# New prices and ranks for the planner of an expert stage, and the last tile's scaling moved behind a branch

## The chip, the cores and the metric

The kernel runs on one core of one Trainium2 chip. The metric is the time of one execution on the device in microseconds, the median of three runs. Five engines work side by side and wait for one another through semaphores: TensorE (PE in the profile; PEld is its loading of weights), VectorE (DVE), ScalarE (ACT), GpSimd (POOL) and SyncE (SP, which here only issues DMAs).

## The reference

Three layers over 2304 tokens of width 512, cut to what matters. All weights and activations are float32.

```python
def reference(...):
    attn = attention(q, k, v, M_prev, z_prev, beta)   # 4 batches, 8 heads, 576 tokens, d 64
    x = attn.transpose(0, 2, 1, 3).reshape(2304, 512)
    # mixture of 8 experts: each token goes to one
    logits = x @ w_gate
    e = argmax(logits, axis=1); gate_w = softmax(logits)[e]
    y = gate_w * (relu(x @ w1[e]) @ w2[e])             # w1 512x1024, w2 1024x512
    # a dense pair of layers
    h = y @ w_in                                       # 512x2048
    return where(h > 0, h, exp(min(h, 0)) - 1) @ w_out # 2048x512
```

## The kernel before

Three stages follow one another, and each is planned apart. The attention ends near 208 us, the expert stage runs to about 498 us, the dense stage takes the rest.

**The expert stage** (`moe`, L1213) works on tiles of 128 tokens, sorted by expert. The program has 23 fixed tiles (`NTM`, numbers 0 to 22). Two more (`NTM` to `NT`) stand in a branch, `tc.If(nt > NTM)` at L1752, that is entered only if the tokens fall so unevenly over the experts that more than 23 tiles are needed; it isn't entered with these inputs. One tile is: fetch 128 rows by index (`gather`, L1172, on POOL), transpose them on PE (L1276), split into a high and a low part (L1197 to L1203), 24 matmuls with w1 (L1337), relu on ACT (L1347, called h), transpose h (L1362), split, 24 matmuls with w2 (L1380), scale by the gate weight (L1393 on ACT or L1396 on DVE), and scatter the rows with an indirect DMA (L1423, after L1419 has put the tokens' numbers beside them).

**Weights.** If a tile has another expert than the tile before it, `tile_weights` (L1158) loads w1 in two DMAs of 1 MB and w2 in two more, and `wsplit` splits them: four steps on ACT (L1312, two casts of 128x1024 each) and four on DVE (L1317, two subtractions each). If it has the same expert, a flag that the chip itself works out makes SP, ACT and DVE jump over that (the branches at L1310 and L1315). So each of these steps is in the program for every tile from 1 on, and whether it costs anything is known on the chip alone.

**Beside the tiles** the stage does three other things: the routing of the last batch (`gate_plan` and `routing`, a chain of small steps on DVE and PE that tells tiles 4 to 22 their tokens), the repacking of the dense stage's weights (`Widen`: 32 parts, each a load into `wide`, one step on ACT at L1116, four on DVE at L1120 to L1132, and a store to `wf`), and the first three loads of these weights back (`first`, L1439).

**What sets the order.** A planner (`Plan`) is given all operations of a stage, each with the engines that may run it, a cost in ns, what it reads and writes, a rank (`prio`, lower goes first) and, for DMAs, a time in a common queue. It plays them through in time: at each step it takes the engine that can start first, and among the operations that can start within `slack` of that the one with the lowest rank. The order so found is each engine's program; on the chip every engine then goes through its own list strictly in order. A tile's rank is 1000 times its number, plus a constant for the kind of operation, plus an offset from the table `moff` in `KNOBS` (for instance "1t2" for the matmuls with w1 of tile 2). `K["load"]` is the DMA time that the planner books for one `tile_weights` call of a tile (default `m_ld`, 3500), `K["same"]` what it books for one weight-splitting step on ACT and on DVE (default `m_if`, 700). Both had own values for tiles 1 to 3 only. "late" and "late2" are the ranks of the last batch's gate and routing. Buffers and PSUM banks are handed out by the same play-through (`Ring`, `Slot`); `released` tells the order in which the PSUM banks come free, and the dense stage takes them in that order.

**The end of the stage.** The last tile's result goes into a bank of the ring for w1's products and is scaled into a corner of a weight buffer. Its scaling, number copy and scatter are part of the plan; the branch at L1752 stands behind the plan in the source.

Of the kernel before, what the change touches and what calls it, by code (L numbers as in the profile page):

```python
# [32 lines left out]
NTM = NT - 2  # L33
# [86 lines left out]
class Plan:  # L120
# [144 lines left out]
KNOBS = {  # L265
    "xe": ("ACT", "DVE"), "he": ("ACT",), "re": [("ACT",), ("ACT", "DVE")], "m_ld": 3500.0, "m_x": -2208.9, "m_1": -1447.9, "m_h": -4434.5, "m_lag": 0.0,
    "m_if": 700.0, "m_fl": -3000.0, "m_wl": 300.0, "wa": 0, "wa0": 10022.449169040721, "wa1": 23927.854833523612, "wt": 1, "wp": 16, "wj": 2000.0,
    "m_g": -500, "wq": 0.64, "sa": 95.3, "sm": 0.0, "s2": 150.0, "hd": -807380.0, "mem": -2415304.4, "xg": 4,
    "wh": [("ACT", "DVE"), ("ACT", "DVE"), ("ACT", "DVE"), ("DVE",), ("ACT",), ("ACT", "DVE"), ("ACT", "DVE"), ("ACT", "DVE")],
    "wl": [("DVE",), ("DVE",), ("DVE",), ("DVE",), ("DVE",), ("DVE",), ("DVE",), ("DVE",)], "ord": [3, 4, 2, 1, 0], "rings": 4, "ab": 2, "nq": 2,  # L270
    "nv": 2, "na": 2, "na4": 2, "nx": 2, "nls": 2, "wide": 1, "de": ("DVE", "POOL"), "busy": [0, 0, 0], "early": -250015.8, "late": 4025.2,
    "late2": 5033.0, "mld": -1956.4, "gate": -150617.9, "warm": [52, 0.0, 200.0], "qe": ("DVE",),
    "off": {"tk": 566796.0, "tq": 730416.0, "hk": -153830.8, "hq": 102000.2, "px": -706093.7, "phi": -153683.4, "S3": -519297.9, "S4": -875790.6, "S2": -808121.2, "S1": -886679.1, "S0": -903722.2, "min3": -650466.1, "min4": -656196.4, "min2": 99641.2, "min1": 773227.1, "min0": -808922.5, "exp3": 834197.7, "exp4": -1722599.5, "exp2": 566072.9, "exp1": 893897.4, "exp0": 608896.6, "T3": 570667.0, "T4": 691939.6, "T2": 562700.4, "T1": 104395.2, "T0": 95607.6, "Te3": -1956.7, "Te4": -370288.3, "Te2": 703913.6, "Te1": 683059.5, "Te0": -888022.2, "fin": -51043.5, "mm": -162856.2, "md": -261207.1, "ms": 171709.6, "avA": -370579.0, "avB": 171831.9, "ave": -150657.8, "rw": -1189064.1, "ls": -697154.8, "add": -705115.8},
    "es": {"x": ("ACT",), "T0": ("ACT", "DVE"), "T3": ("ACT", "DVE"), "k": ("ACT", "DVE"), "T1": ("ACT",), "T4": ("ACT", "DVE"), "q": ("ACT",), "T2": ("ACT", "DVE")},
    "glag": {3: 6500.0}, "begin": {"PE": 300.0, "DVE": 2100.0}, "load": {1: 100.0, 2: 5240.0, 3: 100.0},
    "same": {1: (150.0, 150.0), 2: (1950.0, 2450.0), 3: (150.0, 150.0)},
    "moff": {"x0": 13435.3, "xe0": 22685.2, "fACT0": 17446.5, "fDVE0": 18937.6, "1t0": -19968.7, "r0t0": 11469.5, "r1t0": 8016.8, "h0t0": -12050.5, "h1t0": -7987.2, "he0t0": 10156.1, "he1t0": -756.6, "2t0": -1051.8, "yt0": -3878.6, "w0t0": 4525.5, "w1t0": 19974.4, "w2t0": -21470.7, "w3t0": 59.3, "w4t0": 4555.4, "w5t0": 13589.9, "w6t0": 22393.4, "w7t0": 15561.2, "x1": -1076.0, "xe1": -5940.5, "fACT1": -5210.8, "fDVE1": -246.9, "1t1": -8238.6, "r0t1": 20652.8, "r1t1": -9722.7, "h0t1": -14320.2, "h1t1": 4359.4, "he0t1": -566.2, "he1t1": -2023.2, "2t1": 7927.9, "yt1": 4658.9, "sh0t1": 4642.7, "sh1t1": 6076.0, "sh2t1": 11617.3, "sh3t1": 17594.9, "sl0t1": -800.3, "sl1t1": -8451.5, "sl2t1": -4070.1, "sl3t1": 3393.0, "x2": 4431.3, "xe2": -1464.8, "fACT2": 4958.1, "fDVE2": 5793.9, "1t2": 19111.1, "r0t2": 4317.1, "r1t2": 13362.6, "h0t2": -4316.7, "h1t2": -7360.8, "he0t2": 1487.7, "he1t2": 2315.0, "2t2": 3316.2, "yt2": 11174.7, "sh0t2": 7463.8, "sh1t2": 11468.1, "sh2t2": 19952.2, "sh3t2": 3089.1, "sl0t2": 4551.9, "sl1t2": -15052.7, "sl2t2": 19969.9, "sl3t2": 18614.4, "x3": 6545.5, "xe3": -14606.2, "fACT3": 6360.6, "fDVE3": 4604.0, "1t3": 6547.4, "r0t3": 13373.7, "r1t3": 32874.8, "h0t3": 3850.6, "h1t3": -6823.9, "he0t3": -6525.6, "he1t3": 4650.0, "2t3": -4197.2, "yt3": 13940.6, "sh0t3": 16527.2, "sh1t3": 18722.6, "sh2t3": -18207.3, "sh3t3": -12155.8, "sl0t3": 2292.5, "sl1t3": -5211.1, "sl2t3": 11196.1, "sl3t3": -6237.2},
    "wait": 25, "first": 1042461.7, "stick": 1109662.3,
}

# [215 lines left out]
def ca(n, sb=False, bias=False, acc=False):  # L496
    if acc:
        return 240 + 0.833 * n
    return (110 if sb else 65) + 0.833 * n


def cv(n):
    return 70 + 1.04 * n
# [709 lines left out]
def moe(tc, c, w1, w2, tiles):  # L1213
    nc = tc.nc
    mp, pl, K = c.mp, c.pl, c.K

    def sb(name, n, shape, dt=F32, more=()):
        if name not in c.mt:
            c.mt[name] = [*more] + [mp.tile(shape, dt, name=f"{name}{i}") for i in range(n)]
        return Ring(name, c.mt[name])  # L1220
# [30 lines left out]
    def mtile(t):  # L1251
        pr = 1000.0 * t

        def at(x, y):
            return pr + y + K["moff"].get(f"{x}{t}", 0.0)
# [3 lines left out]
        sg = Slot(r_xg)  # L1259
        if t:  # L1260
            for j in range(2):
                if t == 1 and j == 1:

                    def f():
                        for w in raw[2:]:
                            nc.gpsimd.memset(w[0:1, 0:1], 0.0)
                    pl.op("POOL", 150, f, w=[("raw", 1, 2), ("raw", 1, 3)], prio=pr + K["m_g"])
                tile_weights(tc, c, (w1, w2), t, j, prio=pr - 2900 + 900 * j, dma=K["load"].get(t, K["m_ld"]))
            gather(tc, c, t, lambda: sg.t, r=[("tok", part)] + ([("xd", B - 1)] if part else []), w=[sg], prio=pr - 3000, lag=K["glag"].get(t, 0.0))
        else:  # L1270
            sg.index = r_xg.free.pop(0)[1]
# [115 lines left out]
        if t == NTM - 1:  # L1387
            def f():
                nc.gpsimd.memset(sy.t[:, DM:], 0.0)
            pl.op("POOL", 100, f, w=[("raw", 0, 0), (sy, "id")], prio=pr)  # L1390

        def fa():
            nc.scalar.activation(sy.t[:, 0:DM], y.t, AF.Copy, scale=sg.t[:, DM:DM + 1])  # L1393
# [1 line left out]
        def fv():  # L1395
            nc.vector.tensor_scalar_mul(sy.t[:, 0:DM], y.t, sg.t[:, DM:DM + 1])  # L1396
        es = ("ACT", "DVE") if t < NE else ("ACT",)
        pl.op(es, [{"ACT": ca(512), "DVE": cv(512)}[x] for x in es], [{"ACT": fa, "DVE": fv}[x] for x in es], r=[y, sg], w=[sy], prio=at("yt", 500))

        if t < NE - NY:  # L1400
            def f():
# [13 lines left out]
                  K["he"], ("DVE",))  # L1415
            return

        def f():
            nc.gpsimd.tensor_copy(sy.t[:, DM:DM + 1], c.R.tok[part][:, t - NE:t - NE + 1])  # L1419
        pl.op("POOL", 100, f, r=[sy, ("tok", part)], w=[(sy, "id")], prio=pr + 499)  # L1420

        def f():
            ins = nc.gpsimd.indirect_dma_start(out=c.yd[:, :], out_offset=bass.IndirectOffsetOnAxis(ap=c.R.pos[:, t - NE:t - NE + 1], axis=0),  # L1423
                                               in_=sy.t, in_offset=None, bounds_check=NTOK - NE * P - 1, oob_is_err=False)
            c.no_dep(ins, "y")
        pl.op("POOL", 1040, f, r=[sy, (sy, "id"), "pos", "ypad"], w=[], prio=pr + 500, dma=728, lag=K["m_lag"])

    for t in tiles:
# [216 lines left out]
def kernel(ctx, tc, q, k, v, M_prev, z_prev, beta, w_gate, w1, w2, w_in, w_out, out):  # L1645
# [17 lines left out]
    def released(tiles, rings):  # L1663
        return [next(i for i, x in enumerate(tiles) if x is r.tiles[k]) for _, _, k, r in sorted((t, n, k, r) for n, r in enumerate(rings) for t, k in r.free)]
# [29 lines left out]
    with ExitStack() as s1:  # L1694
# [25 lines left out]
                    wd.part(n, c.K["wa0"] + c.K["wa1"] * n)  # L1720
            phase(build, c.K["sa"], 0.0, **BEGIN)
        with ExitStack() as s2:
            c.mt = {}
            c.mp = Singles(tc, s2)
            c.qone = counts(c.mp, 768)
            for n, k in (("h", 2), ("hh", 2), ("hl", 2)):
# [68 lines left out]
```

## Time and profile before

| | us |
|---|---|
| median of three runs | 912.38 |
| the runs | 911.12 to 916.92 |
| the profiled execution | 913.57 |
| its span, first to last instruction | 911.8 |

The profile is of one execution. The span is what its instructions cover; 1.77 us of the execution lie outside it. A row of the timeline gives start, duration, engine, line of the source, operation, what is written and read, and in brackets how long the engine had stood idle and what it waited for. "x4" means four instructions shown as one row.

### The profile page before, as it was taken

How to read it: one execution, taken by the hardware profiler on the slowest of the kernel's cores; microseconds unless marked ns; L12 is line 12 of the kernel's file. 1: busy time of each engine (PE TensorE's matmuls, PEld its weight loads, DVE VectorE, ACT ScalarE, POOL GpSimd, SP SyncE). 2: the span in 40 equal slices, each digit the busy share in tenths (PEclk: the TensorE clock that was granted, in tenths of full speed). 3: DMA queues.
4: the chain of work that ended last, by engine and by line, in shares of the span. 5: the costliest groups of instructions: out<-in, count | busy, mean ns of one | idle time of the engine just before them, and what ended most of it. 6: DMA issues, size and time to landing. Idle time of an engine off the chain costs nothing.

```text
span 911.8 us, 19048 instructions
## 1 busy us (share of the span) xinstructions
PE 887.9 (97%) x7397; PEld 737.7 (81%) x7397; DVE 571.0 (63%) x1045; ACT 402.5 (44%) x793; POOL 114.2 (13%) x176
## 2 busy tenths in 40 slices
PE   8999999999999999999999999999999999999996
PEld 5777777778788888888887899888888888888895
DVE  5878797979755686468996874444444345344442
ACT  6888888886433574358875331111111112111110
POOL 1111111130001122232111000010001000100100
PEclk9999999999999999999999999999999999999998
DMA  6435353367436883789974620110001000000000
GB/s 120 97 90 130 80 132 69 93 213 243 142 108 220 328 264 129 239 312 372 332 272 171 223 98 13 36 47 0 24 24 47 1 23 24 36 1 1 35 13 23
DMA packets 97108, 110.04 MB, mean 121 GB/s; under 512 B 65390, under 2 KB 65390, under 8 KB 94704
## 3 DMA queue, kind: packets, MB, share of 16 engines
q1 hardware_dynamic: 90992, 95.26, 32.7%
q0 software_dynamic: 4800, 13.18, 4.2%
q8 instruction: 59, 0.97, 0.4%
q10 hardware_dynamic: 1216, 0.30, 0.1%
q14 instruction: 41, 0.34, 0.1%
HBM read 87.94 MB, written 23.41 MB: 122 GB/s over the span
## 4 chain that ended last, share of the span: by engine, by line
PE 68%; DMA 2%; DVE 1%; ACT 1%; issue 0%; POOLq 0%; SPq 0%; POOL 0%; ACTq 0%; DVEq 0%
PE ptt L1607 22%; PE ptt L1582 21%; PE pmt L1380 12%; PE pmt L1337 11%; PE pmt L1362 2%; PE pmt L1276 1%; DMA wide<-wf 1%; DMA half<-wf 1%; PE ptt L1549 1%; DMA ex<-xd,r_tok 0%; DVE wq L1317 0%; ACT h L1347 0%; DVE w L1496 0%; POOLq L1791 0%; ACT wq L1312 0%
## 5 line engine op out<-in xcount | busy, mean ns | idle before, releaser
L1590 ACT ACTIVATE elu<-ptt 128x512 f32<-128x512 f32 x72 | 42.9, 598 | 315.9 <-PE ptt L1582 315.9
L1594 DVE TENSOR_SCALAR elu<-elu 128x512 f32<-128x512 f32 x72 | 31.0, 430 | 187.9 <-ACT elu L1590 187.9
L1607 PE MATMUL ptt<-w,gh 128*128 128x512 f32 x432 | 134.7, 393 | 0.0
L1380 PE MATMUL pmt<-w,hh 128*128 128x512 f32 x368 | 125.0, 400 | 0.0
L1607 PEld LDWEIGHTS ptt<-w,gh 128*128 128x128 f32 x432 | 79.3, 188 | 15.2
L1607 PE MATMUL ptt<-w,gl 128*128 128x512 f32 x216 | 84.2, 390 | 0.0
L710 ACT ACTIVATE a<-pat,st 128x128 f32<-128x128 f32 (+2 forms) x144 | 78.2, 548 | 8.6 <-DVE st L705 5.4
L1380 PEld LDWEIGHTS pmt<-w,hh 128*128 128x128 f32 x368 | 69.1, 188 | 13.4 <-DVE w L1317 0.2
L705 DVE TENSOR_REDUCE st<-pat 128x2 f32<-128x256 f32 (+4 forms) x80 | 64.0, 800 | 19.9 <-PE pat L687 16.5
L1380 PE MATMUL pmt<-w,hl 128*128 128x512 f32 x184 | 71.8, 390 | 0.0
L1582 PE MATMUL ptt<-yTh,w 128*128 128x256 f32 (+1 forms) x288 | 68.8, 318 | 0.0
L1496 DVE TENSOR_TENSOR gl<-tnh,gh 128x512 fp32r<-128x512 f32 x72 | 49.9, 693 | 5.1 <-PE ptt L1607 0.5
L1598 DVE SCALAR_TENSOR_TENSOR tnh<-ptt,elu 128x512 f32<-128x512 f32 x72 | 49.8, 692 | 4.5 <-DVE elu L1594 0.5
L1582 PEld LDWEIGHTS ptt<-yTh,w 128*128 128x128 f32 x288 | 49.2, 190 | 4.0
L827 POOL TENSOR_TENSOR raw<-ms,ls 128x80 f32<-128x80 f32 (+2 forms) x45 | 30.3, 696 | 140.7 <-DVE ls L815 134.6
L1607 PEld LDWEIGHTS ptt<-w,gl 128*128 128x128 f32 x216 | 40.6, 188 | 8.7
L683 PE MATMUL pat<-ab 64*128 64x128 f32 (+3 forms) x256 | 47.0, 473 | 0.2 <-ACT ab L633 0.2
L1582 PE MATMUL ptt<-yTl,w 128*128 128x256 f32 (+1 forms) x144 | 45.8, 318 | 0.0
L1203 DVE TENSOR_TENSOR hl<-pmt,hh 128x512 fp32r<-128x512 f32 x46 | 31.6, 687 | 20.1 <-ACTq L1310 13.2
L1197 ACT CAST hh<-pmt 128x512 fp32r<-128x512 f32 x46 | 27.3, 593 | 36.8 <-PE pmt L1380 28.9
L1347 ACT ACTIVATE h<-pmt 128x512 f32<-128x512 f32 x46 | 27.1, 597 | 37.2 <-PE pmt L1337 35.9
L117 PE MATMUL pat<-ident,a 64*128 64x64 f32 x800 | 36.8, 229 | 5.2 <-ACT a L710 3.9
(343 smaller groups left out, 1932.7 us busy)
## 6 DMA issues: line engine op xcount, KB each, us to landing
wraw<-in_moe_w_dram SPq DMA_DIRECT2D x24, 1024.0 KB, 7.0
wrbw<-in_moe_w_dram SPq DMA_DIRECT2D x12, 1024.0 KB, 7.8
wide<-in_moe_w_in_dram SPq DMA_DIRECT2D x16, 512.0 KB
wf<-half SPq DMA_DIRECT2D x32, 256.0 KB, 4.2
wide<-in_moe_w_out_dram SPq DMA_DIRECT2D x16, 512.0 KB
wide<-wf SPq DMA_DIRECT2D x9, 512.0 KB, 8.4
v<-in_v_dram SPq DMA_DIRECT2D x32, 128.0 KB, 2.9
wraw<-yd SPq DMA_DIRECT2D x14, 258.0 KB, 2.5
```

Source lines behind the costliest of these rows:

```text
L117: nc.tensor.transpose(out, x, ident[hs, hs])
L683: nc.tensor.matmul(s.t[:, 512 * h:512 * h + n], row(1)[hs, i * P:(i + 1) * P], row(0)[hs, 0:n], start=True, stop=False)
L705: nc.vector.tensor_reduce(ss.t[:, 2 * i:2 * i + (2 if i < 4 else 1)], src(), axis=AX.X if i < 4 else AX.XY, op=ALU.min)
L710: nc.scalar.activation(sa[i].t[:, h, :] if i < 4 else sa[4].t[:, 0:S].rearrange("p (y n) -> p y n", y=2), src()[:, h, :] if i < 4 else src ...
L1203: nc.vector.tensor_sub(lo(), src(), hi().bitcast(F32))
L1337: nc.tensor.matmul(g[hf].t, a.t[:, cc, :], b[:, 512 * hf:512 * (hf + 1)], start=(cc == 0 and n == 0), stop=(cc == 3 and n == 2))
L1380: nc.tensor.matmul(y.t, a.t[:, 2 * (q % 2) + jj, :], b[:, 512 * jj:512 * (jj + 1)], start=(q == 0 and jj == 0 and n == 0), stop=(q == 3 an ...
L1496: nc.vector.tensor_sub(lo(), src(), hi().bitcast(F32))
L1582: nc.tensor.matmul(h.t[:, n * j + n0:n * j + n1], w(cc, a, ft), b(cc), start=(cc == 0 and x == 0), stop=(cc == 3 and x == 2))
L1590: nc.scalar.activation(se.t, h.t, AF.Exp)
L1598: nc.vector.scalar_tensor_tensor(st.t, h.t, 0.0, se.t, op0=ALU.max, op1=ALU.add)
L1607: nc.tensor.matmul(acc[a].t, y.t[:, n * j + P * a:n * j + P * (a + 1)], wsub(1, k, ft // 2)[:, ft % 2, :], start=(ft == 0 and x == 0), sto ...
```

## The change

It has five parts, all for the expert stage.

1. Prices. `load` and `same` get own values for tiles 4 to 22 too. Tiles 9, 10, 16, 17, 19, 20 and 22 are booked as new experts (5240 ns of DMA for each of the two `tile_weights` calls, 1950 and 2300 ns for each splitting step on ACT and DVE), the other twelve as repeated ones (100 and 150).
2. Ranks. All offsets in `moff` for tiles 0 to 3 are new, and tiles 4, 20, 21 and 22 get offsets for the first time. The planner's `slack` in this stage (`sm`) goes from 0 to 30 ns, "late" from 4025.2 to 5288.6 and "late2" from 5033.0 to 7126.8.
3. A new memset of one element on POOL, which tile 2's first weight load then waits for.
4. The last tile's scaling, number copy and scatter leave the plan and are issued behind the branch, in the order copy, scaling, scatter.
5. What these three read is held: the PSUM bank of the last result stays taken in the plan and is put at the end of the list that the dense stage takes its banks from, and the row buffer is withheld from the rare tiles.

```diff
-"sm": 0.0, ... "late": 4025.2, "late2": 5033.0,
+"sm": 30.0, ... "late": 5288.6, "late2": 7126.8,
-"load": {1: 100.0, 2: 5240.0, 3: 100.0},
-"same": {1: (150.0, 150.0), 2: (1950.0, 2450.0), 3: (150.0, 150.0)},
+"load": {1: 100.0, 2: 5240.0, 3: 100.0, 4: 100.0, ... 9: 5240.0, 10: 5240.0, ... 22: 5240.0},
+"same": {1: (150.0, 150.0), 2: (1950.0, 2450.0), ... 9: (1950.0, 2300.0), ... 22: (1950.0, 2300.0)},
-"moff": {"x0": 13435.3, ... "1t2": 19111.1, ... "sl3t3": -6237.2},
+"moff": {"x0": 22273.2, ... "1t2": 44312.7, ... "sl3t4": 4255.9, "x20": -14925.1, ... "sl3t22": 6770.1},
@@ moe
+    if c.held is not None:
+        r_xg.free = [x for x in r_xg.free if x[1] != c.held.index]
@@ mtile
+                if t == 2 and j == 0:
+                    def f():
+                        nc.gpsimd.memset(raw[0][0:1, 0:1], 0.0)
+                    pl.op("POOL", 100, f, w=[("raw", 0, 0)], prio=pr - 2950)
@@ t == NTM - 1
             pl.op("POOL", 100, f, w=[("raw", 0, 0), (sy, "id")], prio=pr)
+            y.left += 1
+            c.held = sg
-        pl.op(es, [...], [{"ACT": fa, "DVE": fv}[x] for x in es], r=[y, sg], w=[sy], prio=at("yt", 500))
+        if t != NTM - 1:
+            pl.op(es, [...], [{"ACT": fa, "DVE": fv}[x] for x in es], r=[y, sg], w=[sy], prio=at("yt", 500))
-        pl.op("POOL", 100, f, r=[sy, ("tok", part)], w=[(sy, "id")], prio=pr + 499)
+        if t == NTM - 1:
+            c.tail = [fi, fa, f]
+            return
+        pl.op("POOL", 100, fi, r=[sy, ("tok", part)], w=[(sy, "id")], prio=pr + 499)
@@ tile_attention_moe_mlp_kernel
             late = released(ones, (c.rg, c.rt, c.ry))
+            late += [k for k in range(8) if k not in late]
             nt = nc.values_load(...)
             with tc.If(nt > NTM):
                 ...
+            with tc.manual_schedule():
+                for f in c.tail:
+                    f()
```

## Rows read from the trace of the kernel before

**Rows 1.** The page's first part: busy time, share of the span, instructions.

```profile
PE 887.9 (97%) x7397; PEld 737.7 (81%) x7397; DVE 571.0 (63%) x1045; ACT 402.5 (44%) x793; POOL 114.2 (13%) x176
```

**Rows 2.** Windows of the expert stage; the first row names the columns.

```profile
core 0: us, PE busy (x) PEld busy (x) DVE busy (x) ACT busy (x) POOL busy (x), PEclk, DMA share, GB/s
...
410.00:420.00 10.00, 9.48 (x46) 7.95 (x47) 9.81 (x14) 9.34 (x13) 1.36 (x2) 1.00 1.03 387
...
450.00:460.00 10.00, 10.00 (x47) 8.31 (x46) 9.93 (x12) 8.11 (x12) 3.20 (x3) 1.00 1.01 384
...
480.00:490.00 10.00, 8.89 (x44) 7.11 (x43) 5.24 (x8) 4.23 (x7) 1.35 (x2) 1.00 0.72 262
```

**Rows 3.** Waits of PE, 205 to 520 us: us in total, times, longest.

```profile
PE pmt L1362 <- ACT h L1347: 2.1, 3, 1.1
```

**Rows 4.** The chain that ended last, one undisturbed tile: start us, us, what.

```profile
313.23 4.80 PE pmt L1380 x21
...
325.50 4.79 PE pmt L1380 x21
```

**Rows 5.** Timeline of ACT and of PE around the stalls at 410 and 435 us.

```profile
409.31 0.67 ACT L1116 ACTIVATE half<-wide 128x512 f32<-128x512 f32 x1 [1.73 <-DMA wide<-in_moe_w_out_dram]
...
410.52 0.66 PE L1362 MATMUL pmt<-ident,h 128*128 128x128 f32 x4 [0.66 <-ACT h L1347]
...
433.78 1.25 ACT L1116 ACTIVATE half<-wide 128x512 f32<-128x512 f32 x2
...
435.57 0.66 PE L1362 MATMUL pmt<-ident,h 128*128 128x128 f32 x4 [0.29 <-ACT h L1347]
```

**Rows 6.** Timeline and chain around the stall at 486 us.

```profile
477.45 7.14 DMA wide<-wf
...
484.77 1.04 ACT L1197 CAST wraw1n<-wide 128x1024 fp32r<-128x1024 f32 x1 [2.00 <-DVEq L1315]
...
486.36 1.15 PE L1362 MATMUL pmt<-ident,h 128*128 128x128 f32 x8 [1.11 <-ACT h L1347]
```

**Rows 7.** One splitting step on ACT and DVE (timeline); weight loads (page, part 6).

```profile
427.17 2.00 ACT L1312 CAST w<-wrbw 128x1024 fp32r<-128x1024 f32 x2
...
431.12 2.36 DVE L1317 TENSOR_TENSOR w<-wrbw,w 128x1024 fp32r<-128x1024 f32 x2 [0.45 <-ACT w L1312]
...
wraw<-in_moe_w_dram SPq DMA_DIRECT2D x24, 1024.0 KB, 7.0
wrbw<-in_moe_w_dram SPq DMA_DIRECT2D x12, 1024.0 KB, 7.8
```

**Rows 8.** Timeline of PE and POOL: the stage's first matmuls; tile 4's rows.

```profile
207.65 3.22 PE L1337 MATMUL pmt<-wq,x 128*128 128x512 f32 x12
...
244.91 1.19 POOL L1172 DMA_INDIRECT ex<-xd,r_tok  x1 [32.97 <-DVE r_past L1069]
...
248.57 0.72 PE L1276 MATMUL pmt<-ident,ex 128*128 128x128 f32 x4 [0.60 <-DMA ex<-xd,r_tok]
```

**Rows 9.** Lines L1752 and L1393 (duration ns min/median/max, first and last start); timeline 494 to 509 us.

```profile
L1752 ACTq COMPARE_BRANCH  x1: 50/50/50, 494.0 to 494.0; - x1
...
L1393 ACTq EVENT_SEMAPHORE  x22: 17/38/510, 226.3 to 496.1; - x22
...
494.77 0.50 POOL L1419 CAST wraw<-r_tok 128x1 f32<-128x1 uint32 x1
...
497.91 0.69 ACT L1393 ACTIVATE wraw<-pmt,xs 128x512 f32<-128x512 f32 x1 [2.04 <-PE pmt L1380]
498.66 1.06 PE L1549 MATMUL ptt<-ident,wraw 128*128 128x128 f32 x8 [0.79 <-ACT wraw L1393]
498.67 0.98 SPq L1508 DMA_DIRECT2D half<-wf  x2
```

**Rows 10.** Timeline of POOL and SP at the stage's start.

```profile
205.79 0.09 POOL L1266 MEMSET wrbw<- 1x1 f32 x1
...
206.08 7.31 SPq L1158 DMA_DIRECT2D wraw<-in_moe_w_dram  x2
```

More of the change, by code (lines that the diff above doesn't have):

```diff
@@ L267 @@
     "m_if": 700.0, "m_fl": -3000.0, "m_wl": 300.0, "wa": 0, "wa0": 10022.449169040721, "wa1": 23927.854833523612, "wt": 1, "wp": 16, "wj": 2000.0,
-    "m_g": -500, "wq": 0.64, "sa": 95.3, "sm": 0.0, "s2": 150.0, "hd": -807380.0, "mem": -2415304.4, "xg": 4,
+    "m_g": -500, "wq": 0.64, "sa": 95.3, "sm": 30.0, "s2": 150.0, "hd": -807380.0, "mem": -2415304.4, "xg": 4,
     "wh": [("ACT", "DVE"), ("ACT", "DVE"), ("ACT", "DVE"), ("DVE",), ("ACT",), ("ACT", "DVE"), ("ACT", "DVE"), ("ACT", "DVE")],
@@ L270 @@
     "wl": [("DVE",), ("DVE",), ("DVE",), ("DVE",), ("DVE",), ("DVE",), ("DVE",), ("DVE",)], "ord": [3, 4, 2, 1, 0], "rings": 4, "ab": 2, "nq": 2,
-    "nv": 2, "na": 2, "na4": 2, "nx": 2, "nls": 2, "wide": 1, "de": ("DVE", "POOL"), "busy": [0, 0, 0], "early": -250015.8, "late": 4025.2,
-    "late2": 5033.0, "mld": -1956.4, "gate": -150617.9, "warm": [52, 0.0, 200.0], "qe": ("DVE",),
+    "nv": 2, "na": 2, "na4": 2, "nx": 2, "nls": 2, "wide": 1, "de": ("DVE", "POOL"), "busy": [0, 0, 0], "early": -250015.8, "late": 5288.6,
@@ L273 @@
+    "late2": 7126.8, "mld": -1956.4, "gate": -150617.9, "warm": [52, 0.0, 200.0], "qe": ("DVE",),
     "off": {"tk": 566796.0, "tq": 730416.0, "hk": -153830.8, "hq": 102000.2, "px": -706093.7, "phi": -153683.4, "S3": -519297.9, "S4": -875790.6, "S2": -808121.2, "S1": -886679.1, "S0": -903722.2, "min3": -650466.1, "min4": -656196.4, "min2": 99641.2, "min1": 773227.1, "min0": -808922.5, "exp3": 834197.7, "exp4": -1722599.5, "exp2": 566072.9, "exp1": 893897.4, "exp0": 608896.6, "T3": 570667.0, "T4": 691939.6, "T2": 562700.4, "T1": 104395.2, "T0": 95607.6, "Te3": -1956.7, "Te4": -370288.3, "Te2": 703913.6, "Te1": 683059.5, "Te0": -888022.2, "fin": -51043.5, "mm": -162856.2, "md": -261207.1, "ms": 171709.6, "avA": -370579.0, "avB": 171831.9, "ave": -150657.8, "rw": -1189064.1, "ls": -697154.8, "add": -705115.8},
@@ L274 @@
     "es": {"x": ("ACT",), "T0": ("ACT", "DVE"), "T3": ("ACT", "DVE"), "k": ("ACT", "DVE"), "T1": ("ACT",), "T4": ("ACT", "DVE"), "q": ("ACT",), "T2": ("ACT", "DVE")},
-    "glag": {3: 6500.0}, "begin": {"PE": 300.0, "DVE": 2100.0}, "load": {1: 100.0, 2: 5240.0, 3: 100.0},
-    "same": {1: (150.0, 150.0), 2: (1950.0, 2450.0), 3: (150.0, 150.0)},
-    "moff": {"x0": 13435.3, "xe0": 22685.2, "fACT0": 17446.5, "fDVE0": 18937.6, "1t0": -19968.7, "r0t0": 11469.5, "r1t0": 8016.8, "h0t0": -12050.5, "h1t0": -7987.2, "he0t0": 10156.1, "he1t0": -756.6, "2t0": -1051.8, "yt0": -3878.6, "w0t0": 4525.5, "w1t0": 19974.4, "w2t0": -21470.7, "w3t0": 59.3, "w4t0": 4555.4, "w5t0": 13589.9, "w6t0": 22393.4, "w7t0": 15561.2, "x1": -1076.0, "xe1": -5940.5, "fACT1": -5210.8, "fDVE1": -246.9, "1t1": -8238.6, "r0t1": 20652.8, "r1t1": -9722.7, "h0t1": -14320.2, "h1t1": 4359.4, "he0t1": -566.2, "he1t1": -2023.2, "2t1": 7927.9, "yt1": 4658.9, "sh0t1": 4642.7, "sh1t1": 6076.0, "sh2t1": 11617.3, "sh3t1": 17594.9, "sl0t1": -800.3, "sl1t1": -8451.5, "sl2t1": -4070.1, "sl3t1": 3393.0, "x2": 4431.3, "xe2": -1464.8, "fACT2": 4958.1, "fDVE2": 5793.9, "1t2": 19111.1, "r0t2": 4317.1, "r1t2": 13362.6, "h0t2": -4316.7, "h1t2": -7360.8, "he0t2": 1487.7, "he1t2": 2315.0, "2t2": 3316.2, "yt2": 11174.7, "sh0t2": 7463.8, "sh1t2": 11468.1, "sh2t2": 19952.2, "sh3t2": 3089.1, "sl0t2": 4551.9, "sl1t2": -15052.7, "sl2t2": 19969.9, "sl3t2": 18614.4, "x3": 6545.5, "xe3": -14606.2, "fACT3": 6360.6, "fDVE3": 4604.0, "1t3": 6547.4, "r0t3": 13373.7, "r1t3": 32874.8, "h0t3": 3850.6, "h1t3": -6823.9, "he0t3": -6525.6, "he1t3": 4650.0, "2t3": -4197.2, "yt3": 13940.6, "sh0t3": 16527.2, "sh1t3": 18722.6, "sh2t3": -18207.3, "sh3t3": -12155.8, "sl0t3": 2292.5, "sl1t3": -5211.1, "sl2t3": 11196.1, "sl3t3": -6237.2},
@@ new lines @@
+    "glag": {3: 6500.0}, "begin": {"PE": 300.0, "DVE": 2100.0},
+    "load": {1: 100.0, 2: 5240.0, 3: 100.0, 4: 100.0, 5: 100.0, 6: 100.0, 7: 100.0, 8: 100.0, 9: 5240.0, 10: 5240.0, 11: 100.0, 12: 100.0, 13: 100.0, 14: 100.0, 15: 100.0, 16: 5240.0, 17: 5240.0, 18: 100.0, 19: 5240.0, 20: 5240.0, 21: 100.0, 22: 5240.0},
+    "same": {1: (150.0, 150.0), 2: (1950.0, 2450.0), 3: (150.0, 150.0), 4: (150.0, 150.0), 5: (150.0, 150.0), 6: (150.0, 150.0), 7: (150.0, 150.0), 8: (150.0, 150.0), 9: (1950.0, 2300.0), 10: (1950.0, 2300.0), 11: (150.0, 150.0), 12: (150.0, 150.0), 13: (150.0, 150.0), 14: (150.0, 150.0), 15: (150.0, 150.0), 16: (1950.0, 2300.0), 17: (1950.0, 2300.0), 18: (150.0, 150.0), 19: (1950.0, 2300.0), 20: (1950.0, 2300.0), 21: (150.0, 150.0), 22: (1950.0, 2300.0)},
@@ L1397, in mtile @@
         es = ("ACT", "DVE") if t < NE else ("ACT",)
-        pl.op(es, [{"ACT": ca(512), "DVE": cv(512)}[x] for x in es], [{"ACT": fa, "DVE": fv}[x] for x in es], r=[y, sg], w=[sy], prio=at("yt", 500))
+        if t != NTM - 1:
+            pl.op(es, [{"ACT": ca(512), "DVE": cv(512)}[x] for x in es], [{"ACT": fa, "DVE": fv}[x] for x in es], r=[y, sg], w=[sy], prio=at("yt", 500))
         if t < NE - NY:
@@ L1416, in mtile, with fi @@
             return
-        def f():
+        def fi():
             nc.gpsimd.tensor_copy(sy.t[:, DM:DM + 1], c.R.tok[part][:, t - NE:t - NE + 1])
-        pl.op("POOL", 100, f, r=[sy, ("tok", part)], w=[(sy, "id")], prio=pr + 499)
         def f():
@@ L1722 @@
         with ExitStack() as s2:
-            c.mt = {}
+            c.mt, c.held = {}, None
             c.mp = Singles(tc, s2)
```

1 line of the change is left out of this document (added).

## The prediction

> **What bounds the kernel now.** I read the page first. PE is busy for 97% of the span, the next engine for 63% [rows 1], so the kernel is bound by PE, and a change that takes no work from PE can win only PE's idle time. The diff leaves every matmul and transpose as it was, so I went on to the windows and the waits of PE to find what idle time lies in reach. The change acts on the expert stage alone, from its first matmul at 207.65 [rows 8] to the first transpose of the dense stage at 498.66 [rows 9]. The plans before and after that stretch have the same knobs, and the little that reaches the dense stage (the order of its PSUM banks) is weighed below.
>
> In the chain of waits an undisturbed tile is pure PE: the same run of 21 matmuls starts at 313.23 and at 325.50, so a tile takes 12.27 us and nothing but PE is on its path [rows 4]. What PE loses in the stage are five waits:
>
> - three times the transposes of h (L1362) wait for the relu on ACT: 2.1 us in all [rows 3], 0.66 at 410.5, 0.29 at 435.6 [rows 5] and 1.11 at 486.4 [rows 6];
> - 0.60 at 248.6 for the rows of tile 4 [rows 8];
> - 0.79 at the change of stage, which the profile puts down to the last scaling [rows 9].
>
> That makes 2.06 + 0.60 + 0.79 = 3.45 us. The clock is no part of it: the granted clock was 1.00, the upper of its two levels (2.4 GHz), also in the windows that hold the longest of these waits [rows 2].
>
> **Part 1, the prices.** In all three L1362 waits ACT is late because its list puts something slow ahead of the relu. At 409.31 it is a step of the repacking that stood 1.73 us waiting for its load; at 433.78 two such steps, 1.25 us, are directly ahead [rows 5]; at 484.77 it is a cast of the first dense weights, which followed a load of 7.14 us [rows 6]. An ACT that goes through a list in order can't step over these. The plan put them there because it took them for ready. It booked 3500 ns of DMA for every weight load and 700 ns for every splitting step of tiles 4 to 22, whether the chip does them or jumps over them. The rows show what a real one costs: 2.00 us per step on ACT and 2.36 on DVE [rows 7]. So a tile with a new expert takes 4 x 2.00 = 8.0 us of ACT and 4 x 2.36 = 9.4 of DVE, where 2.8 was booked. The new table books 7.8 and 9.2. Its count of tiles fits: the profile has 24 + 12 = 36 loads [rows 7], which is 4 for tile 0 and 4 for each of eight more, and the table books eight (2, 9, 10, 16, 17, 19, 20 and 22). All three late relus lie after 400 us, where the last five of those eight lie close together, DVE is busy 9.8 and 9.9 of 10 us and the DMAs move 384 to 387 GB/s [rows 2]. No instruction is added or taken away by this part. Its worth lies between nothing (the waits are shifted) and 2.06 us (all three go). I take the 2.06: all three have the one cause that the prices describe.
>
> For the loads the new price is still short. At 387 GB/s, the most that the windows show [rows 2], two loads of 1 MB take 2.097 MB / 387 = 5.4 us, and 5.24 is booked, 0.2 less. A rule speaks more strongly against it: "DMA: Bandwidth & Descriptors" of the Trainium skill, section Specifications, gives some 358 GB/s as one core's share of HBM; 2.097 MB would then take an estimated 5.9 us, and a load would be 0.6 us late against the plan. The rows do not bear that rate out as a ceiling, since their 387 holds reads and writes together; by the rule the second rival below would be the likeliest and the time 912.4.
>
> **Part 2, ranks and slack.** They permute what is ready at the same time; the work is the same. What new order they make can't be read from the trace, so I bound it. Above: a plan of 23 tiles with partly wrong prices left four waits inside the stage, of 0.29 to 1.11 us. Below: none. I take one new wait of the smallest size, 0.3 us, since order made from better prices errs less, but the booked loads are still short. The later rank of the routing is the part that could cost most, and is a rival below; the wait of 0.60 for tile 4, which hangs on it, I leave as it is.
>
> **Part 3, the memset.** One on POOL takes 0.09 us [rows 10]. Tile 2's first load, issued at 206.08, now comes after it. The row shows a start of two issues that spans 7.31 us [rows 10]: SP stands in the second one until about 213, whose buffer is not free. What is queued on SP behind both waits for the second anyway, and tile 2's set of weights is complete only with the second, so a first load that is later by up to some 5 us delays nothing. POOL's own later work moves by the 0.09. Below: nothing to gain. Taken: 0. If that cover were gone, it would cost 0.1 us, or the time for which POOL stands at the memset ahead of it, if it is put behind one that waits.
>
> **Part 4, the tail.** It reads like a move but for ACT it hardly is one. In the trace of before, ACT's branch at L1752 is at 494.0, and the last wait that belongs to L1393 is at 496.1, behind it; the scaling itself starts at 497.91, when PE's last product is there [rows 9]. So it already stood behind the branch in the program. What moves is POOL's copy of 0.50 us, which ran at 494.77, ahead of the end of the branch. Behind it, POOL has from there to 498.60, the end of the scaling, before the scatter can start; the copy fits into that. SP's first load of the dense stage starts at 498.67, as soon as the scaling is done [rows 9], and will again. Taken: 0, with bounds of -0.79 (the wait at the change of stage goes) and +0.5 (the copy comes out of its cover, and what waits for POOL is later by it).
>
> **Part 5, what is held.** One bank less in a ring of four for the last half tile, in which no other product is started; the bank that came free last was last in the list before, too. Taken: 0.
>
> **The sum.** The profiled execution took 913.57. Off go 2.06, on comes 0.3: 913.57 - 1.76 = 911.8. The median of the runs lies 1.19 below the profiled one, so in its measure 912.38 - 1.76 = 910.6.
>
> **Rivals.**
>
> *The plan finds more.* The wait for tile 4 and the one at the change of stage go too: 912.38 - 3.45 = 908.9. For it: the end tiles now have ranks of their own. Against it: a fetch that takes 3.7 us from its issue to the transposes and a branch are no matter of ranks.
>
> *The stretch after 400 us is full, and no order helps.* DVE at 9.8 to 9.9 of 10 and DMAs at a share of 1.01 to 1.03 [rows 2] would mean that a relu's neighbours are late wherever they stand; the waits come back at other places. Time 912.4. Against it: PE lost only 2.06 us there, and the window from 480 us, with the longest wait, has DVE at 5.2 and the DMAs at 0.72 [rows 2].
>
> *Slower: the routing comes too late.* Its rank goes up by 1263 and 2094, where a tile is 1000, so it may fall behind the weight splits on DVE, 2.36 us each. The fetch of tile 4 was issued at 244.91 and PE waited for it [rows 8], though it had other work left: tiles 0 to 3 are 4 x 12.27 = 49 us, to about 257, and some 2 us of the routing's own matmuls. So PE runs dry if the fetch is later by about 259 - 249 = 10 us, less some 2 for transpose and split: from 8 us on, each further one is lost. One tile later is 12.3 us and costs 4.3: 912.38 - 1.76 + 4.3 = 914.9; two tiles cost 16.6, 927. Against it: the planner sees that chain with its true costs and would run dry in its own account.
>
> **How the numbers follow.** Chances: the forecast 0.50, more found 0.15, no help 0.18, routing late 0.12 (of it 0.03 by two tiles), other losses 0.05. The time is that of the forecast, 910.6; its own range is from 910.3 (no new wait) to 911.4 (a new wait of 1.11). The range for all goes from 907.6, which is 908.9 less the 1.3 by which the fastest run of before lies under the median, to 914.9, one tile's delay. About one per cent, 9.1 us, is what a measurement of this kernel can tell from no change. Faster by that is out of reach of 3.45 us of waits: 0.01. Slower by that takes the routing two tiles late or a loss that I haven't seen: 0.04. So 0.95 for within one per cent.
>
> **What would show it.** Right: the PE waits of the expert stage have no L1362 row, or one below 0.5 us in all; the repacking's steps on ACT stand behind the relu of tiles 17, 19 and 22; the transposes of the dense stage start about 1.8 us sooner, near 496.9; the stage's end still has a wait near 0.8. Wrong: the L1362 waits are back at other tiles (no help); the fetch of tile 4 is issued after 253 us with PE idle for microseconds behind it (routing); or the span changes outside 207 to 510 us, where I have the change do nothing.

## The result, and the profile after

The changed kernel took 918.96 us (median of 9 runs, 917.25 to 920.58), the kernel before 912.95 (median of 9, 911.12 to 916.92). The ratio is 1.0059, with a 95% interval from 1.0047 to 1.0070: about 5.4 us slower by the ratio, 6.0 by the medians. That lies outside the predicted range, on the other side than forecast.

The loss sits in one stretch of the expert stage. From its first matmul to the start of its last product the stage took 497.47 - 207.65 = 289.82 us before and 504.82 - 209.85 = 294.97 after, 5.15 more. What lies behind the last product took 414.30 and 413.37. What lies ahead of the stage took 207.65 and 209.85, but its code is the same in all kernels below, and their profiles spread from 207.06 to 209.81 there, so that difference is none of the change. Part of this spread is the clock: in nine of these eleven profiled executions the granted clock has a mean of 0.83 from 20 to 30 us, in those of before and of experiment 8 it is 1.00.

First the waits of PE in the changed kernel, 200 to 510 us (us in total, times, longest):

```profile
PE pmt L1284 <- DMA xs<-xd,r_tok: 4.6, 1, 4.6
PE ptt L1563 <- ACT wraw L1403: 0.7, 1, 0.7
...
PE pmt L1388 <- DVE hl L1204: 0.2, 1, 0.2
```

The lines have moved: the transposes of h are L1370 now, those of x L1284, the relu L1355, the second products L1388, the fetch L1173, the weight loads L1159. In most kernels below the numbers are shifted by some lines; what a row writes and reads tells which step it is (the dense stage's first products, L1582 before, write `ptt` and wait for `tnh`, the end of its activation on DVE). There is no row of L1370 waiting for ACT: the three waits of [rows 3] are gone, and so is the one for tile 4's rows [rows 8]. In their place stands one wait of 4.6 us for fetched rows. The timeline of SP, POOL and PE around it (start us, us, engine, line, what):

```profile
443.39 1.21 SPq L1159 DMA_DIRECT2D wraw<-in_moe_w_dram  x2
...
444.29 1.24 POOL L1173 DMA_INDIRECT xs<-xd,r_tok  x1 [9.46 <-ACTq L1318]
...
447.43 0.39 PE L1345 MATMUL pmt<-ws,xl 128*128 128x512 f32 x1
447.66 0.39 PE L1345 MATMUL pmt<-ws,xh 128*128 128x512 f32 x1
452.62 1.13 PE L1284 MATMUL pmt<-ident,xs 128*128 128x128 f32 x4 [4.57 <-DMA xs<-xd,r_tok]
...
453.97 0.63 PE L1345 MATMUL pmt<-ws,xl 128*128 128x512 f32 x1
454.40 0.63 PE L1345 MATMUL pmt<-ws,xh 128*128 128x512 f32 x1
```

The fetch is the 22nd: it brings the rows of tile 21. PE reaches that tile's transposes at 447.9, some 3.6 us after the fetch was issued, and stands until 452.62. The chain of work says how long the fetch took, 8.28 us from issue to landing:

```profile
444.29 8.28 DMA xs<-xd,r_tok
```

Behind the stand the matmuls start 0.43 us apart (453.97, 454.40), where those of 128x512 ahead of it start 0.23 apart (447.43, 447.66). The windows show why (PEclk is the granted clock in parts of the upper level):

```profile
440.00:450.00 10.00, 8.05 (x36) 6.31 (x34) 8.44 (x11) 4.47 (x6) 3.14 (x3) 1.00 0.66 221
450.00:460.00 10.00, 7.38 (x29) 6.16 (x30) 3.73 (x4) 3.54 (x6) 0.00 (x0) 0.66 0.94 363
```

While PE stood, the clock fell to its lower level (1.2 GHz, where the upper is 2.4). Windows of 0.5 us show it there from about 450.7 to 457.5, and PE was at work in the last 4.9 of these 6.8 us. Start to start, against the usual distance of each pair of instructions, the gap cost 4.73 us and the slow instructions up to 457.4 another 2.38: 7.1 us. "TensorE: Matmul & The Clock Gate" of the Trainium skill, section HAM oscillation, tells the same of a kernel whose TensorE stands for a DMA: its next work begins at the lower clock. This trace agrees, with the 0.66.

The kernel before had that tile's fetch at nearly the same time, and the transposes far behind it (timeline of POOL, SP and PE of before):

```profile
443.18 1.04 POOL L1172 DMA_INDIRECT xs<-xd,r_tok  x1 [9.65 <-ACTq L1310]
...
445.33 1.06 SPq L1158 DMA_DIRECT2D wraw<-in_moe_w_dram  x2
...
459.73 0.63 PE L1276 MATMUL pmt<-ident,xs 128*128 128x128 f32 x4
```

Two things differ. The transposes came 16.55 us after the fetch's issue, not 3.6. And tile 20's second pair of weight loads (2 x 1 MB) was issued 2.15 us behind the fetch, not 0.9 ahead of it. So there were two suspects, the place of the transposes and the order of the transfers, and as a third the edits of the code beside the knobs.

### The profile page after: what moved, and what is told of

Read it like the earlier page. It is cut to its first block, busy times and chain, and to the rows that moved or that the text cites. A ratio compares the mean times of both kernels' runs of the same rounds, so it can differ in the third digit from the quotient of the medians.

```text
span 918.2 us, 19061 instructions
## 1 busy us (share of the span) xinstructions
PE 892.6 (97%) x7397; PEld 740.4 (81%) x7397; DVE 568.8 (62%) x1041; ACT 405.8 (44%) x797; POOL 114.6 (12%) x177
## 4 chain that ended last, share of the span: by engine, by line
PE 50%; issue 18%; POOL 3%; DMA 1%; DVE 0%; POOLq 0%; ACT 0%
PE ptt L1596 22%; PE ptt L1621 21%; PE pmt L1388 3%; POOL yd L1433 2%; PE pmt L1345 2%; DMA xs<-xd,r_tok 1%; PE ptt L1563 1%; POOL y L1430 0%; POOL xs L1173 0%; PE pmt L1370 0%; POOL xg L1173 0%; DVE hl L1204 0%; POOL ex L1173 0%; PE pmt L1284 0%; POOLq L1809 0%
## 5 line engine op out<-in xcount | busy, mean ns | idle before, releaser
L1388 PE MATMUL pmt<-w,hh 128*128 128x512 f32 x368 | 124.9, 401 | 0.0
L1388 PEld LDWEIGHTS pmt<-w,hh 128*128 128x128 f32 x368 | 69.7, 189 | 13.9 <-ACT hh L1198 0.2
L1388 PE MATMUL pmt<-w,hl 128*128 128x512 f32 x184 | 72.1, 392 | 0.2 <-DVE hl L1204 0.2
L1355 ACT ACTIVATE h<-pmt 128x512 f32<-128x512 f32 x46 | 27.5, 598 | 33.0 <-PE pmt L1345 31.4
L1388 PEld LDWEIGHTS pmt<-w,hl 128*128 128x128 f32 x184 | 35.0, 190 | 6.6 <-DVE hl L1204 0.5
```

The costliest lines, as they stand in the source:

```text
L1388: nc.tensor.matmul(y.t, a.t[:, 2 * (q % 2) + jj, :], b[:, 512 * jj:512 * (jj + 1)], start=(q == 0 and jj == 0 and n == 0), stop=(q == 3 an ...
```

## The experiments

Each ratio is to the kernel before on the same chip, with its 95% interval. Stage and rest are, in each profiled execution, the time from the first expert matmul to the start of the last product, and from there to the end.

| kernel | median us | ratio | stage us | rest us |
|---|---|---|---|---|
| before | 912.95 | | 289.82 | 414.30 |
| changed | 918.96 | 1.0059 (1.0047 to 1.0070) | 294.97 | 413.37 |
| 1: tile 21's transposes late again | 917.34 | 1.0041 (1.0026 to 1.0055) | 287.96 | 418.83 |
| 2: load behind the fetch | 913.67 | 0.9997 (0.9984 to 1.0010) | 289.72 | 413.59 |
| 3: matmuls in the gap | 916.34 | 1.0033 (1.0017 to 1.0049) | 292.87 | 413.45 |
| 4: code alone | 914.15 | 0.9999 (0.9982 to 1.0017) | 289.50 | 413.39 |
| 5: 1 and 2 together | 911.00 | 0.9970 (0.9958 to 0.9982) | 288.86 | 414.12 |
| 6: prices alone | 917.50 | 1.0044 (1.0031 to 1.0057) | 290.89 | 415.81 |
| 7: ranks alone | 917.15 | 1.0041 (1.0022 to 1.0061) | 295.81 | 413.23 |
| 8: the fetch's price 5500 | 913.02 | 0.9991 (0.9974 to 1.0007) | 288.30 | 413.45 |
| 9: the fetch's price 3500 | 915.16 | 1.0010 (0.9997 to 1.0023) | 290.59 | 414.52 |

The medians come from three groups of runs, in which the kernel before had medians of 913.38 (1 to 4), 913.09 (5 to 7) and 914.11 (8 and 9); across groups only the ratios compare. Stage and rest are of one execution each; the rest is between 413.2 and 414.3 in the kernels that show no new wait there, so differences of about 1 us in these columns say little.

### 1: the transposes late again

```diff
-    "x21": -5924.1
+    "x21": 0.0
```

> The changed kernel with one knob put back: the rank of tile 21's transposes of x (x21) is 0.0 again instead of -5924.1, which puts them some 7 us (11 products of 0.65 us) later in PE's list. Theory A (the loss is PE standing for the fetch of tile 21, because its transposes were ranked to the very moment at which the plan books the fetch to land): the wait of 4.6 us at 448 goes, PE's granted clock stays at 1.00 there, and the time falls by 4.7 + 2.3 = 7.0 us, from 918.96 to about 912. Theory B (the edits of the code behind the knobs cost the time, the wait is a symptom): time stays within 1.5 us of 919. Theory C (the stretch is full of transfers, the wait only moves): a wait of like size at another tile, time 917 to 919.

The stage did what theory A says: the wait is gone and the stage fell by 294.97 - 287.96 = 7.01 us, to 1.86 below the kernel before. But the time fell by 1.6 only, because the rest grew by 5.46. Theory A was right on the stage and had missed what else the rank does. By the time alone this would pass for theory C (917 to 919, a wait of like size elsewhere), though the wait came in the dense stage and not at another tile. PE's waits and the windows of the dense stage's start:

```profile
PE ptt L1596 <- DVE tnh L1612: 3.7, 1, 3.7
...
506.00:511.00 5.00, 1.28 (x11) 1.08 (x10) 2.40 (x4) 3.00 (x5) 0.00 (x0) 1.00 0.93 333
511.00:516.00 5.00, 5.00 (x27) 4.91 (x28) 4.62 (x10) 3.95 (x5) 0.81 (x3) 0.66 0.73 266
```

The chain that ended last, followed through that wait (start us, us, what):

```profile
501.19 0.61 DVE half L1133
...
501.82 1.96 DMA wf<-half
...
503.80 3.50 DMA half<-wf
...
507.38 1.05 ACT w L1504
...
508.45 1.23 DVE w L1510
509.68 0.35 DVE elu L1608
...
510.12 0.70 DVE tnh L1612
...
510.87 4.63 PE ptt L1596 x24
```

The last part of the repacked dense weights was finished only at 501.8. It is stored (1.96 us), loaded back at once (3.50) and split, and DVE's list has that split ahead of the activation (`elu`, `tnh`) that PE waits for. The plan knew: with x21 at 0.0 it stores the last part at 289.3 us of its own account, 4.5 behind the start of PE's last product; with the changed rank at 281.6. So in that account the early transposes had bought something: the repacking done in time.

### 2: the load behind the fetch

```diff
+                if t == 20 and j == 1:
+
+                    def f():
+                        for w in raw[2:]:
+                            nc.gpsimd.memset(w[0:1, 0:1], 0.0)
+                    pl.op("POOL", 150, f, w=[("raw", 0, 2), ("raw", 0, 3)], prio=pr - 1990)
                 tile_weights(tc, c, (w1, w2), t, j, ...)
```

> The changed kernel with tile 20's second pair of weight loads (w2, 2 x 1 MB) held behind tile 21's fetch by two one-element memsets on POOL; the rank of tile 21's transposes stays early. If the queue is the cause (the fetch's packets stand behind the 2 MB issued 0.9 us ahead of it): the fetch lands about 3.5 us after its issue instead of 8.28, PE's wait at 448 falls from 4.6 to under 0.5 us, the clock stays at 1.00, time about 912 to 913. If the early rank alone is the cause whatever the load does (other transfers keep the DMAs just as full): the fetch still takes 6 us or more, a wait of 2 us or more stays, time 915 to 919.

The fetch's issue to landing and PE's wait (DMA issues, KB and median us to landing; waits of PE; timeline of SP and POOL):

```profile
xs<-xd,r_tok POOLq DMA_INDIRECT x1, 5.0
...
PE pmt L1290 <- DMA xs<-xd,r_tok: 1.3, 1, 1.3
...
445.75 1.11 SPq L1159 DMA_DIRECT2D wraw<-in_moe_w_dram  x2
...
443.09 1.04 POOL L1173 DMA_INDIRECT xs<-xd,r_tok  x1 [9.34 <-ACTq L1324]
```

With the load 2.7 us behind the fetch, the landing came after 5.0 us instead of 8.28. The wait shrank from 4.6 to 1.3, the clock stayed at 1.00, and the stage won back 5.25 us, the whole of the 5.15 lost. The expectation erred in size: 5.0, not 3.5. A store of 256 KB and a load of 512 KB still go beside the fetch; that they make the difference is not shown. So the order of the transfers accounts for about 3.3 us of the landing, and the place of the transposes decides whether PE sees it.

### 3: matmuls in the gap

```diff
         def f():
+            for _ in range(20 if t == 21 else 0):
+                nc.tensor.matmul(wx.t, whi[3][:, 0:P], whi[3][:, 0:512], start=True, stop=True)
             for cc in range(4):
                 nc.tensor.transpose(wx.t[:, cc * P:(cc + 1) * P], sg.t[:, cc:DM:4], c.ident)
```

> The changed kernel with 20 more matmuls of 128x512 (20 x 0.227 = 4.54 us of PE) ahead of tile 21's transposes, into the PSUM bank that these overwrite: PE works where it stood. The result is not touched. If standing made the clock fall: the granted clock stays at 1.00 in the windows from 440 to 460, the matmuls behind the gap start every 0.227 us instead of 0.427, and the time falls by 2.3 us, from 918.96 to about 916.7, though PE has 20 matmuls more. If the clock fell for another reason: it falls again, time 919 to 921.

The windows, and the matmuls behind the gap (timeline of PE):

```profile
440.00:450.00 10.00, 10.00 (x46) 8.27 (x45) 7.48 (x10) 3.78 (x5) 3.03 (x3) 1.00 0.68 224
450.00:460.00 10.00, 10.00 (x50) 8.13 (x49) 5.63 (x7) 6.39 (x9) 0.00 (x0) 1.00 0.89 338
...
452.50 0.39 PE L1347 MATMUL pmt<-ws,xl 128*128 128x512 f32 x1
452.73 0.39 PE L1347 MATMUL pmt<-ws,xh 128*128 128x512 f32 x1
```

PE did 20 matmuls more and the stage was 2.10 us shorter than that of the changed kernel (2.3 expected). The granted clock stayed at 1.00, and the matmuls start 0.23 us apart. So the clock fell because PE stood, and that was a third of the loss. The rest of it, the gap itself, is now filled with work of no use.

### 4: the code alone

The kernel before with the code of the changed one (memset, tail, held bank and buffer) and the whole KNOBS table of before.

> The kernel before with the edits of the code alone (memset ahead of tile 2's first load, last scaling and scatter behind the branch, the held bank and the held buffer) and all knobs as before. My prediction's parts 3 to 5 cost 0 (bounds -0.79 and +0.5): 912 to 913.5, the ratio to before within 0.999 to 1.001. If the edits of the code bear part of the loss (theory B): 915 to 919.

No difference: 0.9999. The relu waits of before are there again (waits of PE):

```profile
PE pmt L1369 <- ACT h L1354: 1.8, 3, 0.9
```

Theory B falls: the interval leaves the code at most 0.18% to either side. The knobs bear the loss, and experiments 2 and 5, which have the code and the new knobs together, aren't slower than before either.

### 5: both edits

The edits of 1 and 2 in one kernel.

> The changed kernel with both edits of the two runs before: x21 back to 0.0, and tile 20's second pair of weight loads held behind tile 21's fetch. In the plan the last repacking part is then stored at 282.7 instead of 289.3 (rank alone) and 281.6 (the changed kernel). If the 3.7 us wait that the dense stage got with the rank alone came from that late last part: no wait at 448, no wait of the dense stage above 0.5 us; the expert stage takes about 288.0 us (as with the rank alone), the rest about 413.5 (as with the load held), and the time is about 911 to 911.8, some 1.8 us below the kernel before. If the dense wait belongs to the late transposes themselves: it is back with 2 us or more, time 914 to 917.

0.9970 with an interval wholly below 1: 2.1 us under its own group's 913.09 (2.7 by the ratio), faster than both kernels. The longest waits of PE from 195 to 560 us:

```profile
PE ptt L1602 <- DVE tnh L1618: 0.8, 1, 0.8
PE pmt L1376 <- ACT h L1361: 0.8, 1, 0.8
```

The big wait of the dense stage is gone with the transposes as late as in 1, so it belonged to the late repacking, as the chain there says. One relu wait of 0.8 and a dense wait of 0.8 have come, which is why stage and rest are 0.9 and 0.6 above what was expected. (The profiled execution took 913.01 us, 2.0 above the median.)

### 6 and 7: prices alone, ranks alone

Both start from the kernel before. 6 takes only the new tables `load` and `same`; 7 takes only `moff`, `late`, `late2` and `sm`.

> The kernel before with the table of prices alone (load, same); ranks, routing's ranks and slack as before. The prediction's Part 1: the three L1362 waits, 2.06 us, go, and nothing comes: 913.2 - 2.06 = about 911. All fetches keep 16 us to their transposes in this plan, so the wait of 4.6 us can't come. Rival (the old ranks don't fit the new prices: the plan itself counts a gap of 3.2 us of PE ahead of the last tile's second products, and the last repacking part comes after them): waits of 2 to 4 us at the last tile or at the start of the dense stage, time 913 to 917.

> The kernel before with the ranks, the routing's ranks and the slack of the new one, and the old prices. Tile 21's transposes stand early here too (3.1 us behind the start of its fetch's issue by the start of the fetch's booked landing, 6.7 us in all), so if the early rank is the cause the wait for the rows of tile 21 is there again, 1.5 to 4.6 us, with the lower clock behind a long one: 914 to 919. If the early place needs the new prices to hurt: no such wait, time 912 to 914.

6 first (the longest waits of PE, 195 to 560 us):

```profile
PE pmt L1381 <- DVE w L1318: 1.4, 1, 1.4
PE ptt L1583 <- DVE tnh L1599: 1.3, 1, 1.3
PE pmt L1363 <- DVE xl L1204: 1.0, 1, 1.0
```

The relu waits for ACT are gone, as the prediction's Part 1 wants it. But others came: the last tile's weights (1.4), the start of the dense stage (1.3), a split (1.0). The second is again behind a late repacking: its last store was issued at 500.26, the first load back at 503.83. Stage and rest of this execution are together 2.6 us above those of before; what makes up the 4.0 beyond that is open. The rival of the expectation holds, 4.0 us slower by the ratio. The prices are truer, and old ranks under truer prices make a worse list.

7 has the waits that the prices were to cure. ACT and PE around 413 us, and the window:

```profile
414.44 0.67 ACT L1116 ACTIVATE half<-wide 128x512 f32<-128x512 f32 x1 [3.02 <-DMA wide<-in_moe_w_out_dram]
415.00 1.08 ACT L1347 ACTIVATE h<-pmt 128x512 f32<-128x512 f32 x2
...
415.64 0.77 PE L1362 MATMUL pmt<-ident,h 128*128 128x128 f32 x4 [1.93 <-ACT h L1347]
...
410.00:420.00 10.00, 8.07 (x35) 6.64 (x34) 7.13 (x9) 5.60 (x9) 1.36 (x3) 0.83 1.02 366
```

A step of the repacking stands 3.02 us for its load, with the relu behind it: the picture of [rows 5], larger, and with the lower clock after it. (The profiled execution took 920.6 us, 3.4 above the median.) Tile 21's transposes, which the new ranks pull forward here too, cost nothing: the fetch was issued at 449.92 and tile 20's load at 453.74, 3.8 us behind it, the rows landed after 3.6 us, and PE came for them 6.5 us after the issue. Both expectations missed: no such wait, yet 0.41% slower.

So neither half is good alone, and the two losses don't add up (0.44% and 0.41%, together 0.59%): each half has faults of its own, and together they have another.

### 8 and 9: the price of the fetch

```diff
-    c.pl.op("POOL", 1040, f, dma=734, **kw)
+    c.pl.op("POOL", 1040, f, dma=5500 if t == 21 else 734, **kw)
```

9 has 3500 in place of 5500. Ranks and load are those of the changed kernel.

> The changed kernel with one price: the fetch of tile 21 is booked at 5500 ns of DMA instead of 734, so that the plan has it land 8.4 us after its start, about what the chip took (8.28 and 7.8 in the runs so far). All ranks, tile 20's load and its place are as in the changed kernel. The plan now puts tile 21's transposes 8.7 us behind the fetch (3.75 before) and stores the last repacking part at 282.6. Theory: the plan lost the time to one price. Then no wait for tile 21's rows above 0.3 us though the load still goes ahead of the fetch, the clock at 1.00, no dense wait above 1 us, time about 911 to 912, below the kernel before. Rival (it takes the load's place in the queue to be mended as well): a wait of 1 us or more there, or a new one of 2 us elsewhere, time 913 to 917.

> As the run before with 3500 ns: the plan puts the transposes 6.7 us behind the fetch. With a landing after 7.8 to 8.3 us, PE should stand 1.1 to 1.6 us there. Such a stand was not followed by the lower clock with the load held behind (1.3 us), so the clock should stay at 1.00 and the time be 1.1 to 1.6 above that of the run before: 912 to 913.5. If the place alone mattered, not the distance: no wait, time as in the run before.

8 and then 9 (landing of the fetch; waits of PE, of which 8 has no row for L1284; the window of 9 in which its wait ends):

```profile
xs<-xd,r_tok POOLq DMA_INDIRECT x1, 7.7
...
PE ptt L1563 <- ACT wraw L1403: 0.8, 1, 0.8
PE pmt L1388 <- ACT hh L1198: 0.4, 1, 0.4
```

```profile
xs<-xd,r_tok POOLq DMA_INDIRECT x1, 8.1
...
PE pmt L1284 <- DMA xs<-xd,r_tok: 1.5, 1, 1.5
PE pmt L1370 <- ACT h L1355: 1.0, 1, 1.0
...
450.00:460.00 10.00, 9.13 (x42) 7.66 (x43) 8.31 (x9) 7.12 (x9) 2.96 (x2) 1.00 1.00 384
```

In both the load is still ahead of the fetch (440.70 against 441.49, and 441.90 against 442.69), and the fetch is as slow as ever. With 8.6 us from issue to use PE doesn't see it (stage 288.30); with 6.5 it stands 1.5 us, within the expected 1.1 to 1.6, and the clock stays. So with 5500 this one price takes back the whole loss, with 3500 most of it. Experiment 8 is level with the kernel before: the 0.9991 can't be told from 1, nor from the forecast 0.998. Whether 8 is as good as 5 is open; their intervals overlap.

## Why the prediction was wrong

**What bounds the kernel** was right as far as it goes: two thirds of the loss came in PE's idle time. The sentence that the clock is no part of it held for before and was carried to after without a reason. It had 2.4 of the 7.1 us.

**Part 1, -2.06.** The mechanism was right: the prices alone take away the relu's waits (experiment 6), the ranks alone leave them (7), and the changed kernel has none. Where the new wait is taken away (experiment 1) the stage is 1.86 us below before, against the -1.76 of the sum. That they are so close is partly luck. The waits that went come to 2.66, the relu's 2.06 and the 0.60 for tile 4's rows, which the sum left standing, so 0.8 came back: PE's short stands in that stage are 0.4 of it, and the other 0.4 is in its busy time and stays open. What failed in this part is its bound. "Between nothing and 2.06" excluded a loss on the ground that no instruction is added. Prices reorder everything that is planned after them, and alone they cost 0.44% (experiment 6). The rate of 387 GB/s was not quite the most, since the window from 300 to 310 us has 394; two loads take 5.3 us by that, not 5.4, and nothing hangs on it.

**Part 2, +0.3.** This is the step that failed. The term measured 7.1 us. With that in place of 0.3 the sum gives 912.38 - 2.06 + 7.1 = 917.4, and 918.0 from the 912.95 of the nine runs, where 918.96 was measured. I bounded new waits by the size of the old ones, 0.29 to 1.11, as if a list could only err as much as the list before it. The old waits were small because they were of one kind: ACT late by one or two steps. A wait for a fetch is sized by another thing, the time from its issue to its landing less the distance to its use. The row for that was in the trace: the fetch of tile 21 and its transposes, 16.55 us apart, a cover that I never wrote down. And the diff had the rank of just these transposes, x21 at -5924 where a tile is 1000. I checked the cover of one fetch, tile 4's, and of no other.

Long landings were nothing new; the short cover was. In experiment 4, which has the knobs of before, tile 17's fetch takes 8.2 us, PE comes for its rows 16.57 us after the issue, and nothing waits (timeline of POOL and PE; issue to landing):

```profile
393.51 1.04 POOL L1172 DMA_INDIRECT xs<-xd,r_tok  x1 [9.53 <-ACTq L1317]
...
410.08 0.63 PE L1283 MATMUL pmt<-ident,xs 128*128 128x128 f32 x4
...
xs<-xd,r_tok POOLq DMA_INDIRECT x1, 8.2
```

The plan's own account shows how the cover went. The prediction held that the new order can't be read from the trace and bounded it; but the planner is part of the kernel's source, and played through it gives the start of every operation. It has the fetch start at 231.30, its rows ready at 234.91, and the transposes at 235.05: 0.14 us to spare. It books 734 ns of DMA for a fetch. On the chip the fetch took 8.28 us where the plan has 3.6, and the load that stands 0.6 us behind it in the plan was issued 0.9 ahead: SP and POOL go through lists of their own, and nothing ties the two. That swap is 3.3 of the 4.7 us (experiment 2); what the other 1.4 are is open. And it takes ranks and prices together: with the ranks alone (7) the load came 3.8 us behind the fetch, and PE came 6.5 us after the fetch's issue. Experiments 8 and 9 confirm it: with the one price set to what the chip took, the wait goes; halfway there, what is left of it is the difference.

**Parts 3 to 5, 0.** Right within what can be told: 0.9999, with 1.6 us to either side (experiment 4). The wait at the change of stage was 0.7 and stayed, as in the bound I took. But Part 4's picture was wrong. POOL's copy did not come behind the branch: though it is issued behind it in the source, it ran at 482.26, with POOL's branch at 496.7, where before it ran at 494.77, just behind POOL's branch at 494.2. Why, no run here shows.

```profile
482.26 0.18 POOL L1430 CAST wraw<-r_tok 128x1 f32<-128x1 uint32 x1
```

**The rivals.** *The plan finds more* was half right: the wait for tile 4 did go, the one at the change of stage didn't. *The stretch is full* named the right stretch, and saw late transfers only as something that keeps relus late. *The routing too late* had the right form, a fetch that comes after PE needs it, at the wrong tile: tile 4's fetch moved from 37.3 us behind the stage's first matmul (244.91) to 38.8 (248.62), and cost nothing. No rival took up the other side of that form, that the use comes sooner. It fell under the 0.05 for other losses. And a change of one per cent is not the least that can be told: nine runs of each gave an interval of 0.12% to either side.

**What would show it.** The dense stage's transposes were to start near 496.9; they started at 505.93. The missing L1362 rows were a right sign of Part 1 and no sign of the time. A list of signs that names only the waits that should go can't see the one that comes.

## What to carry to other kernels

When a change moves ranks in a planned list, write down for every fetch how far its use lies behind its issue, and compare that with the longest landing in the trace, not the usual one. A use that is planned to the very moment at which a transfer is booked to land is a stall as soon as another queue's transfer gets ahead. And prices and ranks of one planner are one thing: here each half alone was about 0.4% slower, and mending one price, that of the fetch, took back what both together lost.

## What the runs showed of the hardware

A fetch's landing depends on what else is under way, by more than its own size says: that of tile 21, 258 KB in every kernel, landed after 3.6 us (experiment 7), 5.0 (2) and 8.28 (the changed kernel). In the changed kernel the software queue (q0), in which POOL's fetch runs, moved no packet from its issue at 444.29 until 450, while the hardware queue (q1) was at work. Packets, MB and share of the 16 engines, 448 to 450 us and then 450 to 453:

```profile
q1 hardware_dynamic: 242, 0.48, 94.2%
...
q1 hardware_dynamic: 318, 0.63, 66.0%
q0 software_dynamic: 150, 0.42, 36.5%
```

With the load held behind, q0 had its packets from 446 on, 3 us after the issue. "DMA: Bandwidth & Descriptors" of the Trainium skill, section Queues, rings and completion order, says that the engines take turns between queues, packet by packet; by that rule alone the fetch would have shared q1's time from the start. The trace shows a late start instead, and only then the sharing. Which step of the start is held up, no run here shows.

The granted clock stayed at 1.00 behind stands of 1.3 us (experiment 2), 1.4 (6) and 1.5 (9), and a stretch at the lower level came with those of 1.9 (7), 3.7 (1) and 4.6 us (the changed kernel, where it began while PE still stood). In the longest of them this was a third of the loss.
